# Two more first products inside retention, own banks for the first k, and raw weights touched three steps behind their load

## The chip, the cores and the metric

The kernel runs on one core of one Trainium2 chip. The metric is the device time of one execution in microseconds (us); the kernel before takes 892.86 us, the median of three runs. PE is TensorE, DVE VectorE, ACT ScalarE, POOL GpSimd, SP the engine that issues most of the DMAs.

## The reference

Retention (attention with a decay in place of the softmax) over 4 batches, 8 heads, 576 positions, head size 64, followed by two feed-forward layers on the 2304 tokens it leaves:

```python
scores = scale * np.matmul(q, k.transpose(0, 1, 3, 2))
ret = scores * Dmat                      # Dmat: gamma ** (i - j) at and below the diagonal, else 0
x = np.matmul(ret, v)                    # -> 2304 tokens x 512
h = x @ w_in                             # moe: 512 -> 2048
x = (h * np.tanh(softplus(h))) @ w_out   # mish, 2048 -> 512
g = x @ w_gate; val = x @ w_val          # moe2: 512 -> 1536
out = (g * sigmoid(g) * val) @ w_out2    # 1536 -> 512
```

q, k and v are 32-bit floats; the weights come as 64-bit floats.

## The kernel before, in words

Every product of the feed-forward layers is made in three passes: a matrix is split into a rounded upper part and the lower part that is left, and upper x upper, upper x lower and lower x upper are added up in PSUM.

**Retention** (`retention`) runs over 20 steps t: in each of 4 batches five chunks of 128, 128, 128, 128 and 64 positions. A step t makes scores (`scores`, L505), masks them on DVE into p (L515), transposes k of step t + 1 and q of a later chunk through the PSUM tile `tt` (`turn`, L436), adds the state's part and the own part to the output o (L575, L585), updates the state (L549), and lets DVE scale o into x (L598). POOL scales v for the next step (L493). The first 384 tokens of x are split into `xs` (L365 on ACT, L370 on POOL).

**Weights.** w_in and w_out come in 32 blocks of 512 KB (16 each), in the order of the list `todo`; block j lands in one of `RAW = 4` raw tiles (`fetch`, L102). A block becomes a unit by these operations: `rebias` (ACT L114, DVE L115: a shift), `sign` (DVE L119), `join` (DVE L123), and `part` (ACT L133 casts the upper part, then L134 subtracts for the lower part; POOL does it in retention, DVE in the slots). A raw tile is free for block j + 4 when the part of block j is made. In retention a step does at most one such row of operations, in a step of `REST` none, for at most `NA = 18` units; `rebias` there is done for a block that was loaded two converting steps earlier (`seen`).

**First products.** `g1(s)` multiplies tokens by block i of w_in (12 matmuls, L682), `mish` and `g_hi` (ACT L733, L740) and `g_lo` (DVE L744) make g from it, `g2(s)` multiplies g by block i of w_out and adds into four accumulators (12 matmuls, L716). In retention `g1` runs at the steps of `EARLY`, its mish, `g_hi` and `g_lo` one step later. After retention `slot(s)` does, for s from len(EARLY) to 31, one `g1(s)` and one `g2(s - 4)`, then mish and g, and behind them in the queues the conversions: as many as are needed to have 2s units, and then 1 or 2 more (`weights`). Slots 0 to 15 are the first 384 tokens and slot 16 begins the next; unit 28 is the block of w_out that `g2(12)` reads, which stands first in slot 16. In `todo` the blocks are ordered so that slot s needs units 2s - 4 and 2s - 3.

**Behind them** come the remaining products, with sums of weight blocks made on DVE and written to DRAM (`plain1`, `third`, `second`) while the slots run. All queues run in the order in which the program is written.

Of the kernel before, what the change touches and what calls it, by code (L numbers as in the profile page):

```python
# [7 lines left out]
F32 = mybir.dt.float32  # L8
# [9 lines left out]
def retention_mish_swiglu(  # L18
# [33 lines left out]
    RATES, AHEAD = (2.9, 3.3, 0.4, 1.28, 0.9, 1.0), 45  # L52
    EARLY = (9, 11, 14, 17)
    REST = (9, 14, 18, 19)

# [327 lines left out]
    def retention(g1, mish, g_hi, g_lo):  # L383
        with ExitStack() as c0:
# [40 lines left out]


            def turn(name, *items):
                items = [x for x in items if x]
                if not items:
                    return  # L430
                p = ps1.tile([128, 2, 2, NP, 64], F32, tag="tt", name=f"t{name}")
                for z, (n, src, _) in enumerate(items):
                    for pr in range(NP):
                        for r in range(-(-n // 64)):
                            own = slice(64 * r, min(64 * r + 64, n))
                            nc.tensor.transpose(p[:, r, z, pr, :own.stop - own.start], src(pr)[own], ident[own, own])  # L436
                for z, (_, _, empty) in enumerate(items):
                    empty(p[:, :, z])

            def q_item(b, g, e, eng=nc.scalar.copy):  # L440
# [42 lines left out]
            def q_next(t):  # L483
                b, sc, n = steps[t]
                due = (b, 1, sc) if sc < 2 else (b, 2, 0) if sc == 2 else (b + 1, 0, sc - 3)
                return q_item(*due) if b or sc > 1 else None

# [80 lines left out]
            def output(t):  # L568
                b, sc, n = steps[t]
                o = ps1.tile([128, NP, 128], F32, tag="o", name=f"o{t}")  # L570
                if sc:
                    for pr in range(NP):
                        for e in range(2):
                            own = slice(64 * e, 64 * e + 64)
                            nc.tensor.matmul(  # L575
                                o[own, pr, :n], lhsT=sbd[:, pr, own], rhs=q_cols(t)[:, pr],
                                start=(pr == 0), stop=False, skip_group_check=True,
                            )
                state(t)
                if t == 1:  # L580
                    turn("q0_1", q_item(0, 1, 0), q_item(0, 1, 1))
                state_out(t)
# [51 lines left out]
            warm(W[1])  # L634
            turn("k0", k_item(0))
            scale_v(0)
            warm(W[2])
            for t in range(len(steps)):
                scores(t)
# [12 lines left out]
                if on:  # L652
                    join(stage[2])
                    stage[2] += 1
                if conv:
                    if stage[1] < seen[0]:
                        rebias()
                    seen[:] = seen[1], stage[0]
                if x:
# [10 lines left out]
                if conv:  # L670
                    load_next(NA)
            while stage[3] < stage[2]:
                part(NA)

    with tc.manual_schedule():
# [70 lines left out]
        def slot(s):  # L746
# [20 lines left out]
            if s < F1 + OFF and not parts:  # L767
                for _ in range(1 + s % 2):
                    run(weights(n1, True))
            if s == len(EARLY):  # L770
                plain1(0)
            if s % 2 and s > len(EARLY) and s // 2 - 1 < F1 // 2:
                plain1(s // 2 - 1)
            if stage[3] >= n1:
# [297 lines left out]

        FIN1 = (6, 8, 8, 8, 6, 6, 6)
        for s in range(len(EARLY), NS):
            slot(s)
            if s == NS - F1 + 2:
                ya, yb = ysteps("e0", xt[NC], xt[NC + 1])
                ahead += ya + yb[0] + yb[1]
            if s > NS - F1 + 2:
                pop(ahead, 1 + s % 2)  # L1080
            if s >= NS - F1 + 10:
                stream1(s - (NS - F1 + 10))
# [329 lines left out]
```

## Time and profile before

| | |
|---|---|
| median of 3 runs | 892.86 us (890.14 to 893.03) |
| the profiled execution | 894.11 us, its span 892.3 us |
| PE busy | 871.9 us, 98% of the span |
| DVE, ACT, POOL busy | 652.9, 426.6, 53.1 us |
| granted clock of TensorE, mean | 0.998 |

The span runs from the first to the last instruction; the time of the execution is 1.8 us longer. Busy times are sums over stages with different limits, so where a change falls matters: retention lasts to about 106 us, the slots in which weights are still converted to about 161 us.

### The profile page before, as it was taken

The numbers are of one execution on the slowest core, as the hardware profiler recorded it, in microseconds if no ns is written. First come the engines' busy times: TensorE is split into PE (matmuls) and PEld (weight loads), VectorE is DVE, ScalarE is ACT, GpSimd is POOL, SyncE is SP. The second block draws the span as 40 slices with busy tenths as digits, with TensorE's granted clock in tenths as the row PEclk, the third lists the DMA queues.
The fourth block names the chain that finished last, engine by engine and source line by source line (L and its number), as shares of the span: only waits on it lengthen the run. The fifth ranks groups of instructions, "written<-read, shape, count | busy, mean of one in ns | idle before, by whom it ended". The sixth has DMA issues, their size and how long they took to land.

```text
span 892.3 us, 16688 instructions
## 1 busy us (share of the span) xinstructions
PE 871.9 (98%) x6330; PEld 842.0 (94%) x6330; DVE 652.9 (73%) x1271; ACT 426.6 (48%) x835; POOL 53.1 (6%) x47
## 2 busy tenths in 40 slices
PE   7888999999999999999999999999999999999998
PEld 7777899999999999999999999999999999999998
DVE  3886788998777786777786878876676776575772
ACT  3776566645656556565664424263212263222260
POOL 3654300000000000000000000000000000000000
PEclk9999999999999999999999999999999999999999
DMA  9999578577899985799978698978877878877773
GB/s 210 253 231 250 155 209 263 177 236 252 303 325 315 338 285 165 235 335 342 320 269 280 214 335 310 306 245 274 295 251 244 250 252 270 291 256 252 251 246 119
DMA packets 161600, 232.21 MB, mean 260 GB/s; under 512 B 48240, under 2 KB 124272, under 8 KB 161520
## 3 DMA queue, kind: packets, MB, share of 16 engines
q1 hardware_dynamic: 159984, 229.94, 81.4%
q10 hardware_dynamic: 1536, 1.21, 0.5%
q8 instruction: 50, 0.82, 0.4%
q14 instruction: 30, 0.25, 0.1%
HBM read 178.68 MB, written 52.43 MB: 259 GB/s over the span
## 4 chain that ended last, share of the span: by engine, by line
PE 85%; DVE 5%; DMA 5%; ACT 3%; issue 1%; POOL 1%; SPq 0%; ACTq 0%; POOLq 0%; DVEq 0%
PE t L904 29%; PE T L1298 15%; PE te L904 12%; PE e0a L975 7%; PE e1a L975 6%; PE h L682 5%; PE acc L716 4%; DMA raw<-in_moe_w_out_dram 3%; PE s L505 1%; DMA raw<-in_moe_w_in_dram 1%; PE o L585 1%; PE acc L950 1%; DMA v<-in_v_dram 1%; PE idle L630 1%; PE o L575 1%
## 5 line engine op out<-in xcount | busy, mean ns | idle before, releaser
L904 PE MATMUL t<-y,su 128*128 128x384 f32 x1512 | 267.6, 337 | 0.7 <-DVE u L911 0.4
L904 PEld LDWEIGHTS t<-y,su 128*128 128x128 f32 x1512 | 263.8, 188 | 2.9 <-DVE u L911 0.7
L904 PE MATMUL te<-ye,eu 128*128 128x384 f32 x672 | 136.1, 337 | 0.5 <-DVE scratch L911 0.5
L1298 PE MATMUL T<-su,g 128*128 128x256 f32 x1134 | 135.7, 282 | 0.0
L1298 PEld LDWEIGHTS T<-su,g 128*128 128x128 f32 x1134 | 135.6, 190 | 0.0
L904 PEld LDWEIGHTS te<-ye,eu 128*128 128x128 f32 x672 | 113.5, 188 | 5.0 <-DVE scratch L911 0.7
L975 PE MATMUL e1a<-ge,u 128*128 128x512 f32 (+1 forms) x384 | 76.2, 337 | 0.0
L975 PE MATMUL e0a<-ge,u 128*128 128x512 f32 (+1 forms) x384 | 76.1, 337 | 0.0
L682 PE MATMUL h<-xs,u 128*128 128x384 f32 x384 | 72.2, 337 | 0.0
L975 PEld LDWEIGHTS e1a<-ge,u 128*128 128x128 f32 x384 | 61.9, 188 | 6.0
L975 PEld LDWEIGHTS e0a<-ge,u 128*128 128x128 f32 x384 | 62.0, 188 | 5.8
L682 PEld LDWEIGHTS h<-xs,u 128*128 128x128 f32 x384 | 66.8, 188 | 0.3
L716 PE MATMUL acc<-g,u 128*128 128x384 f32 x336 | 63.4, 337 | 1.5 <-DVE u L134 0.9
L716 PEld LDWEIGHTS acc<-g,u 128*128 128x128 f32 x336 | 58.6, 188 | 2.4 <-DVE u L134 1.5
L1167 ACT ACTIVATE sg<-sg 128x384 f32<-128x384 f32 x54 | 28.4, 525 | 58.5 <-DVE sg L911 58.5
L1196 ACT COPY p<-t 128x384 f32<-128x384 f32 x35 | 16.5, 473 | 80.7 <-PE t L904 80.7
L1130 ACT CAST g<-ga 128x384 fp32r<-128x384 f32 x72 | 32.5, 514 | 43.2 <-DVE ga L1175 32.4
L911 DVE TENSOR_TENSOR u<-t,p 128x384 f32<-128x384 f32 x36 | 20.1, 557 | 40.3 <-PE t L904 40.2
L914 DVE TENSOR_TENSOR g<-ga,g 128x384 fp32r<-128x384 f32 x72 | 36.2, 553 | 6.4 <-ACT g L1130 6.2
L911 DVE TENSOR_TENSOR scratch<-te,scratch 128x384 f32<-128x384 f32 x48 | 26.7, 555 | 13.0 <-PE te L904 10.3
L911 DVE TENSOR_TENSOR v<-t,p 128x384 f32<-128x384 f32 x36 | 20.1, 557 | 17.0 <-PE t L904 16.9
L114 ACT ACTIVATE raw<-raw 128x512 f32<-128x512 f32 x32 | 22.1, 692 | 17.7 <-DMA raw<-in_moe_w_out_dram 12.5
(169 smaller groups left out, 1199.5 us busy)
## 6 DMA issues: line engine op xcount, KB each, us to landing
su<-comb SPq DMA_DIRECT2D x126, 512.0 KB, 4.3
su<-fcomb SPq DMA_DIRECT2D x63, 512.0 KB, 4.2
eu<-ecomb SPq DMA_DIRECT2D x56, 512.0 KB, 5.5
comb<-c SPq DMA_DIRECT2D x48, 256.0 KB, 4.8
raw<-in_moe_w_in_dram SPq DMA_DIRECT2D x16, 512.0 KB, 5.8
raw<-in_moe_w_out_dram SPq DMA_DIRECT2D x16, 512.0 KB, 5.4
ecomb<-e SPq DMA_DIRECT2D x32, 256.0 KB, 2.8
ecomb<-u SPq DMA_DIRECT2D x24, 256.0 KB, 4.6
```

The costliest lines, as they stand in the source:

```text
L114: nc.scalar.activation(hi.bitcast(F32), hi.bitcast(F32), AF.Copy, scale=2.0 ** -112)
L505: nc.tensor.matmul(s[:n, e, pr, :n], lhsT=kT[t][64 * e:64 * e + 64, pr, :n], rhs=q_cols(t)[64 * e:64 * e + 64, pr], start=True, stop=True,)
L682: nc.tensor.matmul(ps, lhsT=u[:, a, kk * 128:(kk + 1) * 128], rhs=s[:, e, :], start=(c == 0), stop=(c == n - 1),)
L716: nc.tensor.matmul(accs[b][d][:, :T], lhsT=u[:, a, d * 128:(d + 1) * 128], rhs=g[:, e, :], start=(i == 0 and c == 0), stop=(i == F1 - 1 an ...
L904: nc.tensor.matmul(p, lhsT=w[:, (high, 1 - high)[a], kk * 128:(kk + 1) * 128], rhs=y[kk][:, x, :], start=begin and kk == 0 and (a, x) == ( ...
L911: nc.vector.tensor_tensor(out=out_, in0=a, in1=b_, op=ALU.add)
L914: nc.vector.tensor_tensor(out=out_, in0=a, in1=b_, op=ALU.subtract)
L975: nc.tensor.matmul(o, lhsT=u[:, a, d * 128:(d + 1) * 128], rhs=y[:, :512] if r == 0 else y[:, 512:], start=f == 0 and (a, x) == (0, 0) and ...
L1130: nc.scalar.copy(out=gt[n, c, i][:, 0], in_=x)
L1167: nc.scalar.activation(x, bank_ if part_ is None else x, AF.Silu)
L1196: (nc.scalar.copy if n or i or z else nc.vector.tensor_copy)(out=r["p1"], in_=p)
L1298: nc.tensor.matmul(p[m], lhsT=g[:, x, m * 128:(m + 1) * 128], rhs=w[:, 1 - a, :], start=begin and i == 0 and (a, x) == (0, 0) and not (sha ...
```

## The change

1. The first k is transposed into two PSUM tiles of its own (`first_k`, tags o and st) and copied out by ACT and DVE, half each; before it went through `tt` behind the first q.
2. The second q chunk of batch 0 is turned in two pieces, one with k of step 2 and one ahead of the state update of step 1, instead of both behind it.
3. `EARLY` has six steps, 8, 10, 12, 14, 16, 18, instead of four; `REST` has five. The slots begin at s = 6, and `g2(0)` and `g2(1)` stand in front of them. Slots up to 8 run two conversions behind their g instead of one or two by turns, and plain weights are sent one odd slot later.
4. In retention a block is rebiased when it was loaded three or more steps earlier (`asked`), from step 3 on.

```diff
-    EARLY = (9, 11, 14, 17)
-    REST = (9, 14, 18, 19)
+    EARLY = (8, 10, 12, 14, 16, 18)
+    REST = (9, 13, 17, 18, 19)
...
+            def halves(n, src, to):
+                for pr in range(NP):
+                    for r in range(-(-n // 64)):
+                        own = slice(64 * r, min(64 * r + 64, n))
+                        nc.tensor.transpose(to(r, pr)[:, :own.stop - own.start], src(pr)[own], ident[own, own])
...
+            def first_k():
+                n, src, _ = k_item(0)
+                p = [ps1.tile([128, NP, 64], F32, tag=tag, name=f"tk0_{tag}") for tag in ("o", "st")]
+                halves(n, src, lambda r, pr: p[r][:, pr])
+                kT[0] = at.tile([128, NP, 128], F32, tag="kT", name="kT0")
+                for r, copy in enumerate((nc.scalar.copy, nc.vector.tensor_copy)):
+                    copy(out=kT[0][:, :, 64 * r:64 * r + 64], in_=p[r])
...
-                due = (b, 1, sc) if sc < 2 else (b, 2, 0) if sc == 2 else (b + 1, 0, sc - 3)
-                return q_item(*due) if b or sc > 1 else None
+                due = (b, 1, sc if b else 0) if sc < 2 else (b, 2, 0) if sc == 2 else (b + 1, 0, sc - 3)
+                return q_item(*due) if b or sc else None
...
+                if t == 1:
+                    turn("q0_1", q_item(0, 1, 1))
                 state(t)
-                if t == 1:
-                    turn("q0_1", q_item(0, 1, 0), q_item(0, 1, 1))
...
-            turn("k0", k_item(0))
+            first_k()
...
-                if conv:
-                    if stage[1] < seen[0]:
-                        rebias()
-                    seen[:] = seen[1], stage[0]
+                if conv and t > 2 and stage[1] < asked[t - 3]:
+                    rebias()
...
+                asked.append(stage[0])
+            seen[0] = asked[-2]
...
-                for _ in range(1 + s % 2):
+                for _ in range(2 if s < len(EARLY) + 3 else 1 + s % 2):
                     run(weights(n1, True))
...
-            if s % 2 and s > len(EARLY) and s // 2 - 1 < F1 // 2:
-                plain1(s // 2 - 1)
+            if s % 2 and s > len(EARLY) and s // 2 - 2 < F1 // 2:
+                plain1(s // 2 - 2)
...
+        for s in range(len(EARLY) - LAG):
+            g2(s)
         for s in range(len(EARLY), NS):
             slot(s)
```

What this does to the order on the engines is shown at three places. In names, the digits up to the underscore say which step, block or product it is, the rest is a running number; lines of the changed kernel lie 12 or 13 further down from retention on.

First DVE in retention, steps 2 to 5, before: x is the scaled output of a step, p the masked scores, raw0 and raw1 the first raw blocks.

```order
L598 TENSOR_TENSOR x0_314<-o2_440,gout_186 128x4x128
L115 TENSOR_SCALAR raw0_324<-raw0_324 128x512
L515 TENSOR_TENSOR p3_487<-s3_478,mask_184 128x2x256 x2
L119 SCALAR_TENSOR_TENSOR raw0_324<-raw0_324 128x512
L598 TENSOR_TENSOR x1_539<-o3_512,gout_186 128x4x128
L123 SCALAR_TENSOR_TENSOR raw0_324<-raw0_324 128x512
L115 TENSOR_SCALAR raw1_406<-raw1_406 128x512
L515 TENSOR_TENSOR p4_562<-s4_553,mask_184 64x2x2x64 x2
```

The same place now:

```order
L610 TENSOR_TENSOR x0_316<-o2_442,gout_186 128x4x128
L527 TENSOR_TENSOR p3_487<-s3_478,mask_184 128x2x256 x2
L610 TENSOR_TENSOR x1_538<-o3_511,gout_186 128x4x128
L115 TENSOR_SCALAR raw0_326<-raw0_326 128x512
L527 TENSOR_TENSOR p4_560<-s4_551,mask_184 64x2x2x64 x2
L119 SCALAR_TENSOR_TENSOR raw0_326<-raw0_326 128x512
L610 TENSOR_TENSOR x1_538<-o4_587,gout_186 128x4x64
L123 SCALAR_TENSOR_TENSOR raw0_326<-raw0_326 128x512
L115 TENSOR_SCALAR raw1_408<-raw1_408 128x512
```

The shift of raw0 (L115) stood behind the x of step 2 and now stands behind that of step 3, and each later block moves a step with it.

Second SP's queue from the load of k for step 8 on, before (q, k, v are loads for retention, raw a weight block):

```order
L418 DMA k8_620<-in_k_dram 128x8x64
L102 DMA raw4_622<-in_moe_w_in_dram 128x4x256
L418 DMA v8_691<-in_v_dram 128x8x64
L405 DMA q10_693<-in_q_dram 128x8x128
L418 DMA k9_695<-in_k_dram 64x8x64
L102 DMA raw5_697<-in_moe_w_out_dram 128x1024
L418 DMA v9_774<-in_v_dram 64x8x64
L418 DMA k10_776<-in_k_dram 128x8x64
```

The same place now:

```order
L418 DMA k8_615<-in_k_dram 128x8x64
L418 DMA v8_684<-in_v_dram 128x8x64
L405 DMA q10_686<-in_q_dram 128x8x128
L418 DMA k9_688<-in_k_dram 64x8x64
L102 DMA raw4_690<-in_moe_w_in_dram 128x4x256
L418 DMA v9_767<-in_v_dram 64x8x64
L418 DMA k10_769<-in_k_dram 128x8x64
L102 DMA raw5_771<-in_moe_w_out_dram 128x1024
```

Block 4 has moved behind v8, q10 and k9, and every later block is behind loads that it stood ahead of; in front of v19 stand blocks 0 to 11 now, 0 to 13 before.

Third DVE where retention ends, before: x5 is the last output, g4 the lower part of the products 4 and 5, u the lower part of a unit.

```order
L598 TENSOR_TENSOR x5_1538<-o19_1696,gout_186 128x4x64
L744 TENSOR_TENSOR g4_1762<-m4_1760,g4_1762 128x384
L119 SCALAR_TENSOR_TENSOR raw13_1469<-raw13_1469 128x512
L115 TENSOR_SCALAR raw14_1545<-raw14_1545 128x512
L123 SCALAR_TENSOR_TENSOR raw13_1469<-raw13_1469 128x512
L744 TENSOR_TENSOR g4_1762<-m5_1799,g4_1762 128x384
L119 SCALAR_TENSOR_TENSOR raw14_1545<-raw14_1545 128x512
L134 TENSOR_TENSOR u13_1804<-raw13_1469,u13_1804 128x512
L115 TENSOR_SCALAR raw15_1626<-raw15_1626 128x512
L123 SCALAR_TENSOR_TENSOR raw14_1545<-raw14_1545 128x512
L119 SCALAR_TENSOR_TENSOR raw15_1626<-raw15_1626 128x512
```

The same place now:

```order
L610 TENSOR_TENSOR x5_1552<-o19_1700,gout_186 128x4x64
L757 TENSOR_TENSOR g4_1623<-m5_1718,g4_1623 128x384
L757 TENSOR_TENSOR g6_1794<-m6_1792,g6_1794 128x384
L115 TENSOR_SCALAR raw10_1396<-raw10_1396 128x512
L119 SCALAR_TENSOR_TENSOR raw10_1396<-raw10_1396 128x512
L115 TENSOR_SCALAR raw11_1470<-raw11_1470 128x512
L123 SCALAR_TENSOR_TENSOR raw10_1396<-raw10_1396 128x512
L134 TENSOR_TENSOR u10_1805<-raw10_1396,u10_1805 128x512
L119 SCALAR_TENSOR_TENSOR raw11_1470<-raw11_1470 128x512
L115 TENSOR_SCALAR raw12_1557<-raw12_1557 128x512
L123 SCALAR_TENSOR_TENSOR raw11_1470<-raw11_1470 128x512
L134 TENSOR_TENSOR u11_1814<-raw11_1470,u11_1814 128x512
```

Before, retention left 13 units (0 to 12) with their parts, and blocks 13 to 15 go on here, one sign and one shift further; now it leaves 10, and blocks 10 to 12 have everything still to be done here, behind the g of product 6.

## Rows read from the trace of the kernel before

**Rows 1.** busy by stage: us, engines' busy (instructions), clock, DMA share, GB/s
```profile
0.00:11.76 11.76, 8.06 (x61) 7.48 (x61) 1.87 (x3) 3.09 (x4) 1.38 (x6) 1.00 1.00 195
11.76:54.60 42.84, 37.03 (x688) 32.44 (x688) 32.06 (x48) 27.44 (x55) 27.35 (x23) 1.00 1.10 245
54.60:106.43 51.83, 47.48 (x781) 42.43 (x777) 38.54 (x60) 35.08 (x68) 24.39 (x20) 0.97 0.87 209
106.43:160.81 54.38, 52.88 (x300) 51.99 (x301) 44.13 (x82) 33.83 (x61) 0.00 (x0) 1.00 0.75 233
160.81:230.00 69.19, 69.19 (x400) 69.19 (x400) 61.74 (x125) 39.10 (x76) 0.00 (x0) 1.00 0.71 231
```

**Rows 2.** waits of PE up to 160 us: us in total, times, longest
```profile
PE o L585 <- DVE p L515: 8.1, 9, 2.2
...
PE s L505 <- DVE qT L456: 1.3, 2, 0.9
```

**Rows 3.** timeline of the start: start, us, engine, line [idle before <-releaser]
```profile
8.62 1.40 DVE L456 COPY qT<-tq 64x512 f32<-64x512 f32 x2 [7.23 <-ACT qT L456]
...
10.28 0.47 PE L436 MATMUL tk<-ident,k 64*128 64x64 f32 x8 [2.10 <-DVE qT L456]
...
11.76 1.16 PE L505 MATMUL s<-qT,kT 64*128 64x128 f32 x16
```

**Rows 4.** chain that ended last, up to 165 us: start us, us, what
```profile
43.20 7.41 DMA raw<-in_moe_w_out_dram
...
144.02 5.61 DMA raw<-in_moe_w_out_dram
```

**Rows 5.** timeline of all engines in retention, 50 to 56 us
```profile
51.11 0.43 DVE L115 TENSOR_SCALAR raw<-raw 128x512 uint32<-128x512 uint32 x1 [1.57 <-DMA raw<-in_moe_w_out_dram]
...
54.10 2.02 DVE L123 SCALAR_TENSOR_TENSOR raw<-raw 128x512 uint32<-128x512 uint32 x1
...
54.25 1.31 POOL L134 TENSOR_TENSOR u<-raw,u 128x512 fp32r<-128x512 f32 x1
```

**Rows 6.** timeline of PE at the end of retention and in the slots
```profile
106.36 2.35 PE L682 MATMUL h<-xs,u 128*128 128x384 f32 x12
108.54 2.24 PE L716 MATMUL acc<-g,u 128*128 128x384 f32 x12
110.62 2.24 PE L682 MATMUL h<-xs,u 128*128 128x384 f32 x12
...
158.79 2.19 PE L716 MATMUL acc<-g,u 128*128 128x384 f32 x11 [0.61 <-DVE u L134]
```

**Rows 7.** timeline of DVE in the slots
```profile
109.81 0.56 DVE L744 TENSOR_TENSOR g<-m,g 128x384 fp32r<-128x384 f32 x1 [2.91 <-ACT g L740]
110.29 0.69 DVE L119 SCALAR_TENSOR_TENSOR raw<-raw 128x512 uint32<-128x512 uint32 x1
...
114.45 0.69 DVE L119 SCALAR_TENSOR_TENSOR raw<-raw 128x512 uint32<-128x512 uint32 x1
115.05 0.69 DVE L134 TENSOR_TENSOR u<-raw,u 128x512 fp32r<-128x512 f32 x1
115.65 0.42 DVE L115 TENSOR_SCALAR raw<-raw 128x512 uint32<-128x512 uint32 x1
115.99 0.69 DVE L123 SCALAR_TENSOR_TENSOR raw<-raw 128x512 uint32<-128x512 uint32 x1
...
117.42 0.69 DVE L134 TENSOR_TENSOR u<-raw,u 128x512 fp32r<-128x512 f32 x1
...
127.96 0.56 DVE L744 TENSOR_TENSOR g<-m,g 128x384 fp32r<-128x384 f32 x1 [0.59 <-ACT g L740]
...
158.05 0.69 DVE L134 TENSOR_TENSOR u<-raw,u 128x512 fp32r<-128x512 f32 x1
```

**Rows 8.** timeline of the DMA queue of SP in retention
```profile
87.72 1.21 SPq L418 DMA_DIRECT2D k<-in_k_dram  x1
```

**Rows 9.** DMA issues up to 110 us: count, KB each, median us to landing
```profile
k<-in_k_dram SPq DMA_DIRECT2D x16, 256.0 KB, 6.2
```

More of the change, by code (lines that the diff above doesn't have):

```diff
@@ L432, in turn @@
                 for z, (n, src, _) in enumerate(items):
[L433 to L436, printed above, removed]
+                    halves(n, src, lambda r, pr: p[:, r, z, pr])
                 for z, (_, _, empty) in enumerate(items):
                     empty(p[:, :, z])
+            def first_k():
[5 more added lines that the diff above has]
+                    copy(out=kT[0][:, :, 64 * r:64 * r + 64], in_=p[r])
             def q_item(b, g, e, eng=nc.scalar.copy):
@@ L634, in retention @@
             warm(W[1])
-            turn("k0", k_item(0))
+            first_k()
             scale_v(0)
             warm(W[2])
+            asked = []
             for t in range(len(steps)):
```

## The prediction

> **What bounds the kernel now.** I read the busy time by stage first [rows 1]. From 160.81 us on TensorE (PE) is busy for the whole stretch to 230 us, so anything that delays PE before that point is paid one for one at the end. The idle time lies ahead of it. Up to 106.43 us (retention) PE is busy 8.06 + 37.03 + 47.48 = 92.6 us and idle 13.9; in the slots up to 160.81 us it is idle 1.5. The share of the whole span (98%) hides this.
>
> Then the waits of PE [rows 2]: 8.1 us in nine waits of the output matmuls for the masked scores p, which VectorE (DVE) writes, and 1.3 us for the q copies. Next the start [rows 3]: the first k transposes wait 2.10 us until the q copies have emptied their bank, and scores begin at 11.76 us.
>
> Why p is late shows in one example [rows 4, 5]: a raw block issued at 43.20 us lands 7.41 us later; DVE gets to it at 51.11 us after a wait of 1.57 us, and p stands behind it in the same queue. A touch one step later would fall at about 54.10 us, when the block is there.
>
> Retention's loads are a second limit: 245 GB/s at a DMA share of 1.10 from 11.76 to 54.60 us [rows 1].
>
> In the slots [rows 6] PE alternates products of 2.08 us (108.54 to 110.62). The last wait that ends there is at 158.79 us, for a lower part written on DVE at 158.05 us [rows 6, 7]. That is unit 28, read by the first second product of slot 16. So the time of the kernel is set by when DVE has converted unit 28, and the whole change comes down to this: when is that unit ready afterwards?
>
> **The change, part by part.** R is the end of retention on PE, 106.36 us before [rows 6]; R' is the same point after.
>
> *First k in own banks.* The 2.10 us wait goes. The first half of k is copied on ScalarE (ACT) while DVE still copies q to 10.02 us (8.62 + 1.40) [rows 3]; the other half takes some 0.4 us behind it (an estimate: half the columns of one q copy, 0.70). Scores can start at about 10.45 instead of 11.76: 1.3 us.
>
> *Two more first products.* Each is 2.28 us of PE (the 2.35 of its row less what overlaps its neighbours) [rows 6]: +4.6 us in retention, and 4.2 us less in the slots. By itself that is no gain; it only pays where PE would have been idle.
>
> *Touch three steps behind.* PE's busy time in retention becomes 92.6 + 4.6, less about 1.5 because the stretch to 106.43 us ran at a granted clock of 0.97 [rows 1]: 95.7. The start's idle time, 11.76 - 8.06 = 3.7, becomes 2.4, and so R' cannot be under 98.1. Of the other 10.2 us of idle I keep 3 (copies, the mish chain, early loads): **R' = 101**. If every wait stayed, R' would be 106.4 + 4.6 - 1.3 = 109.7. Are the loads in the way? SP's order shows that fewer raw blocks now stand ahead of the same q, k, v loads: 12 instead of 14 ahead of the last v. The last k, issued at 87.72 us, moves some 2 x 0.52 MB / 245 GB/s = 4.3 us forward and lands about 6.2 us after issue [rows 1, 8, 9], near 90 us, before its step. So the loads do not hold the end of retention.
>
> *What the later touch costs.* A raw tile is now held one step longer, there are still four of them, and five steps instead of four convert nothing. GpSimd (POOL) therefore makes the lower part of 10 units in retention instead of 13. Units 10, 11 and 12 are still to be touched at all. These three conversions have no cover: they go to the slots, where DVE was the engine waited for.
>
> *The first slot.* DVE stands still longer. Before, its first conversion step came at 110.29 us, 3.93 us after the first product began at 106.36 [rows 6, 7]. Now two second products (4.16 us) come ahead of that product, and the conversions still stand behind its mish in DVE's queue: R' + 8.1. From there I add up DVE's new order with the distances of its old rows: 0.60 us each for sign, join and part, 0.34 for the shift (115.65 to 115.99), 0.48 for g (109.81 to 110.29), and 0.83 between the end of a join and the part of the same unit (115.99 + 0.60 to 117.42, while ACT casts) [rows 7].
> Unit 10: 0.34 + 0.60 + 0.34 + 0.60 + 0.83 + 0.60 = 3.3, done at R' + 11.4. Unit 11 and unit 12: 3.0 each, R' + 17.4. Unit 13: shift, join, g, sign, shift, join, part and 0.3 for its cast: 3.9, R' + 21.3. Before, unit 13 was done at 115.05 + 0.60 = R + 9.3. The chain starts 12 us later relative to the end of retention.
>
> *From unit 13 to unit 28.* Before: 115.05 to 158.05, 43.0 us for 15 units. It holds six waits of 0.6 us for g of a product that PE had not finished (the one at 127.96 us is a sample) [rows 7]; these end when PE is the late one, which gives 39.4. Loads into the four tiles hold it too: one stood in the chain for 5.61 us [rows 4], and this does not get better. I take the middle, 41.2. Bounds: DVE's own work alone, 15 units x (3 x 0.60 + 0.34) + 10 g x 0.48 = 36.9, and 43.0.
>
> *Also changed at no cost:* the sends of plain weights one slot later (SP is not waited for), the split turn for the second q block (saves part of the 1.3 us of [rows 2], counted above).
>
> **Sum.** Unit 28 is done at R' + 21.3 + 41.2 = 101 + 62.5 = 163.5, before at 158.05 + 0.60 = 158.65: 4.8 us later, and everything behind it is unchanged. The profiled execution took 894.1 us, which is 1.2 above the median 892.9; on the median: **897.5 us**. Ends: 98.1 + 21.3 + 36.9 = 156.3, 2.4 us sooner (890.5); with R' at 106.4 and 43.0, 170.7, 12 us later (905).
>
> One price more can be read in two ways. The join at 54.10 us takes 2.02 us while POOL works on a part from 54.25 [rows 5]; in the slots, without POOL, the same operation takes 0.69 [rows 7]. Three POOL parts fewer could so free DVE in retention by up to 3 x 1.31 us. I take nothing for it: PE's long waits there end with a load. The Trainium skill, page "SBUF — State Buffer", section "Who interferes with whom", says that a DVE instruction with two SBUF inputs and a GpSimd instruction that reads SBUF block each other for a whole instruction. By that rule the gain is real, R' falls to its floor, 98.1, and the time is 894.6. The trace agrees that the join is stretched, 2.02 against 0.69 us.
>
> **The rivals.**
> (1) *Not slower: DVE at its own pace in the slots.* If loads never hold it and waits for g vanish, units 13 to 28 take 36.9 us: 101 + 58.2 = 159.2, 0.5 us later: 893.4; with R' at its floor 890.5. For it: four tiles were kept filled at 233 GB/s in that stretch, under the 245 of retention [rows 1]. Against: a load's 5.61 us in the chain [rows 4]. It decides from about 2.6 us per unit down (forecast 2.75, before 2.87).
> (2) *Retention is not shortened.* PE waits as before, now for k and v or for ACT, which has two more mish and casts to do: R' near 106. 106 + 62.5 = 168.5: 902.7. For it: DMA is full to 54.60 us. Against: the raw blocks that are no longer loaded, and the example of [rows 4, 5].
> (3) *DVE in retention is freed* by the missing POOL parts: R' = 98.1, 160.6, 2 us later: 894.6, no change that can be told.
>
> **How the numbers follow.** Forecast 0.5, its own range 894.5 to 901; rival 1 0.22; rival 2 0.16; rival 3 0.12. About 0.3% (2.7 us) is what a measurement of this kernel can tell. Faster by more needs rival 1 with an early R': 0.16. Within it: the rest of rival 1, rival 3 and the low edge of the forecast: 0.24. Slower: 0.60. The range leaves out about one in ten on each side: 889.5 to 904.
>
> **What would show it.** Scores begin near 10.5 us. No wait of DVE for a raw load in retention. PE ends retention between 98 and 104 us, with six first products in it. DVE idle some 7 us around that point; its first shift about 8 us after it. PE waits for u in nearly every slot from slot 7 on, some 15 us in all instead of 1.5 (62.5 us less two second products and ten slots of 4.16); the last wait ends near 163 us, and PE is without gaps behind it. I would be wrong if PE's waits in the slots sum to under 11 us with retention ending by 100, or if PE still waits 8 us for p in retention.

## The result, and the profile after

The changed kernel takes 901.22 us (median of four runs, 899.64 to 902.06), the kernel before 892.70 on the same chip (four runs, 890.14 to 893.03): a ratio of 1.0098, 95% interval 1.0080 to 1.0117, so 8.5 us slower. The profiled executions took 901.48 and 894.11 us; the difference between these two, 7.4 us, is the one that the rows can explain. The median of before in these four runs lies 1.4 us under its profiled execution, that of the changed kernel 0.3 under its own; this is the other 1.1.

Stages of the changed kernel (us, then busy us of each engine with its instructions, granted clock, DMA share, GB/s), as in [rows 1]:

```profile
0.00:10.46 10.46, 7.82 (x61) 7.28 (x61) 2.29 (x4) 2.89 (x4) 1.25 (x5) 1.00 0.97 193
10.46:54.00 43.54, 39.72 (x734) 35.22 (x734) 29.81 (x46) 28.27 (x57) 27.73 (x24) 1.00 1.11 245
54.00:103.60 49.60, 47.61 (x755) 43.34 (x755) 34.43 (x53) 31.48 (x63) 18.20 (x16) 0.97 0.81 191
103.60:166.20 62.60, 52.05 (x269) 46.85 (x265) 48.98 (x90) 34.41 (x61) 0.00 (x0) 0.97 0.65 202
```

The reader sees retention end on PE at 103.60 us instead of 106.36 with two first products more in it, and the slots stretch to 62.6 us with PE idle for 10.5 of them, where it was idle 1.5 before.

Waits of PE up to 103.6 us in the changed kernel (us in total, times, longest), to be held against [rows 2]:

```profile
PE t L431 <- DMA k<-in_k_dram: 3.3, 4, 1.0
...
PE o L597 <- DVE p L527: 0.5, 1, 0.5
```

The waits for p, 8.1 us before, are down to 0.5. Waits for loads of k, of which there were none, stand in their place, 3.3 us.

PE's timeline in the changed kernel: the start, the last late k and the first product behind it, the end of retention, the first unit that came late, and the last:

```profile
10.46 1.16 PE L517 MATMUL s<-qT,kT 64*128 64x128 f32 x16 [1.19 <-DVE kT L450]
...
56.35 0.46 PE L431 MATMUL t<-ident,k 64*128 64x64 f32 x8 [0.95 <-DMA k<-in_k_dram]
...
56.99 3.92 PE L695 MATMUL h<-xs,u 128*128 128x384 f32 x12
...
103.60 4.43 PE L729 MATMUL acc<-g,u 128*128 128x384 f32 x24
...
114.58 4.20 PE L695 MATMUL h<-xs,u 128*128 128x384 f32 x12 [2.39 <-ACT u L133]
...
166.21 2.19 PE L729 MATMUL acc<-g,u 128*128 128x384 f32 x11 [0.68 <-DVE u L134]
```

The last row answers to that at 158.79 us in [rows 6]: the same product, first of slot 16, waits for the same unit 28, 7.42 us later. Profiled time less this row is 901.48 - 166.21 = 735.27 us here and 894.11 - 158.79 = 735.32 before. So the time behind slot 16 did not change; all of the loss is in front of it.

DVE's timeline behind the end of retention and at unit 28, as in [rows 7] (L757 the lower part of g, L115 the shift, L134 the lower part of a unit):

```profile
111.21 0.56 DVE L757 TENSOR_TENSOR g<-m,g 128x384 fp32r<-128x384 f32 x1 [6.60 <-ACT g L753]
111.69 0.42 DVE L115 TENSOR_SCALAR raw<-raw 128x512 uint32<-128x512 uint32 x1
...
114.56 0.69 DVE L134 TENSOR_TENSOR u<-raw,u 128x512 fp32r<-128x512 f32 x1 [0.71 <-ACT u L133]
...
124.07 1.50 DVE L134 TENSOR_TENSOR u<-raw,u 128x512 fp32r<-128x512 f32 x2
...
165.47 0.69 DVE L134 TENSOR_TENSOR u<-raw,u 128x512 fp32r<-128x512 f32 x1
```

DVE stands still for 6.60 us ahead of the g of product 6 (111.21), touches unit 10 at 111.69 (8.1 us behind the end of retention), begins its part at 114.56, that of unit 13 at 124.07 (the row merges it with that of unit 14), and that of unit 28 at 165.47.

### The profile page after: what moved, and what is told of

Its sections match the earlier page's. It is cut to its first block, busy times and chain, and to the rows that moved or that the text cites. A ratio compares the mean times of both kernels' runs of the same rounds, so it can differ in the third digit from the quotient of the medians.

```text
span 899.7 us, 16678 instructions
## 1 busy us (share of the span) xinstructions
PE 875.6 (97%) x6330; PEld 842.2 (94%) x6330; DVE 653.9 (73%) x1275; ACT 426.3 (47%) x835; POOL 47.2 (5%) x44
## 4 chain that ended last, share of the span: by engine, by line
PE 86%; DVE 6%; DMA 3%; ACT 2%; issue 1%; SPq 1%; DVEq 0%; ACTq 0%
PE t L917 29%; PE T L1313 15%; PE te L917 12%; PE e0a L988 7%; PE e1a L988 6%; PE h L695 6%; PE acc L729 4%; DMA raw<-in_moe_w_out_dram 2%; PE o L597 1%; DMA k<-in_k_dram 1%; PE s L517 1%; PE o L587 1%; PE acc L963 1%; DVE raw L123 1%; PE t L431 1%
## 5 line engine op out<-in xcount | busy, mean ns | idle before, releaser
L695 PE MATMUL h<-xs,u 128*128 128x384 f32 x384 | 77.3, 350 | 4.5 <-ACT u L133 2.7
L695 PEld LDWEIGHTS h<-xs,u 128*128 128x128 f32 x384 | 69.2, 196 | 7.8 <-ACT u L133 3.8
L757 DVE TENSOR_TENSOR g<-m,g 128x384 fp32r<-128x384 f32 x32 | 18.4, 575 | 15.8 <-ACT g L753 15.6
```

What stands on the lines that cost most here:

```text
L695: nc.tensor.matmul(ps, lhsT=u[:, a, kk * 128:(kk + 1) * 128], rhs=s[:, e, :], start=(c == 0), stop=(c == n - 1),)
L757: nc.vector.tensor_tensor(out=g[:, 1, :], in0=ws.pop(s), in1=g[:, 0, :].bitcast(F32), op=ALU.subtract)
```

## The experiments

All times are medians of four to twelve runs, each beside runs of the kernel before on the same chip; the chips differ, so kernels are compared by their ratios; "last wait" is the row of the first second product of slot 16, and R' the end of retention on PE, both of the profiled execution. The theories: **A**, the units that retention leaves undone are the loss, because DVE begins them late and has no room to catch up; **B**, the two added first products are; **C**, the later touch brings nothing in retention; **D**, the pace of DVE or of the loads in the slots, and not the start, sets the end.

| kernel | time, us | ratio to before (95%) | R' | last wait | units from retention |
|---|---|---|---|---|---|
| before | 892.70 | 1 | 106.36 | 158.79 | 13 |
| changed | 901.22 | 1.0098 (1.0080 to 1.0117) | 103.60 | 166.21 | 10 |
| e1: changed, old touch | 897.07 | 1.0062 (1.0049 to 1.0074) | 105.79 | 161.85 | 12 |
| e3: before, new touch | 895.35 | 1.0040 (1.0026 to 1.0053) | 99.89 | 158.74 | 10 |
| e4: changed, conversions first | 895.02 | 1.0035 (1.0023 to 1.0048) | 102.79 | 159.81 | 10 |
| e6: e1, conversions first | 891.17 | 0.9992 (0.9981 to 1.0003) | 104.43 | 154.80 | 12 |
| e2: before, first k and split q | 890.77 | 0.9985 (0.9975 to 0.9995) | 104.32 | 155.78 | 13 |
| e8: e6, late parts on POOL | 894.49 | 1.0025 (1.0014 to 1.0036) | 106.33 | 161.21 | 12 |
| e9: e1, two steps in every slot | 898.13 | 1.0071 (1.0056 to 1.0085) | 104.69 | 153.39 | 12 |
| e10: e9, 13 units from retention | 895.19 | 1.0028 (1.0018 to 1.0039) | 104.06 | none | 13 |
| e11: e10, xs first | 886.48 | 0.9943 (0.9928 to 0.9958) | 106.08 | none | 13 |
| e12: e11, slot 13 empty too | 887.09 | 0.9952 (0.9938 to 0.9966) | 107.00 | none | 13 |
| e13: changed, k ahead of q | 899.83 | 1.0094 (1.0080 to 1.0108) | 102.03 | 164.85 | 10 |
| e14: changed, with all of it | 893.68 | 1.0016 (1.0002 to 1.0030) | 103.55 | 154.80 | 10 |

Before, e3 and e2 have four first products in retention and so 4.2 us more of PE behind R' than the others. R' is that of a single execution: e10, e11 and e12 have the same retention and end it at 104.06, 106.08 and 107.00 us, so a difference of one to three us in R' between two kernels is not shown by it alone. Profiled executions also differ in where they lie: those of e8, e11 and e12 are the slowest of their runs, that of e9 the fastest. In e14 the last wait is for unit 27. In the nine kernels whose last wait is for unit 28 and that have no wait behind it at slot 16, the profiled time less that row is 734.8 to 735.3 us, whatever was changed in front.

**e1, the changed kernel with the old touch.**

```diff
-            asked = []
...
-                if conv and t > 2 and stage[1] < asked[t - 3]:
-                    rebias()
+                if conv:
+                    if stage[1] < seen[0]:
+                        rebias()
+                    seen[:] = seen[1], stage[0]
...
-                asked.append(stage[0])
-            seen[0] = asked[-2]
```

> The changed kernel with the old rule for the touch (two converting steps behind the load); six first products and own banks stay. By its order retention leaves 12 units instead of 10. Theory A (the loss is that DVE converts too late after retention: start behind slot 6, and fewer units done): DVE's waits for raw loads come back in retention, so it ends later than 103.6, near 106.5 us; unit 13 is done about 15.0 us after that instead of 21.1 and unit 28 near 163, against 166.1: 897 us, 894 to 900. Theory B (two more first products in retention are the loss as such, units do not matter): no gain, and the raw waits come on top: 902 to 905.

Measured 897.07 us, as theory A had it; DVE waits for raw blocks in retention again, 4.7 us in all. **e3, the kernel before with the new touch alone** (the same lines the other way round):

> The kernel before with only the touch three steps behind the load; four first products, k through the shared bank. Retention leaves 10 units instead of 13. Theory A: retention ends near 100.3 us (103.6 less two products of 2.28, plus 1.3 for the start), six earlier than before, and the chain of conversions is three units longer behind it, some 8 us: unit 28 near 159.3 against 158.65 before, so the gain is eaten: 893.5 us, 890 to 897. Theory C (the touch brings nothing, loads hold retention): it ends near 106 and the three units cost 8 us in full: 901.

Measured 895.35 us. PE in e3, the end of retention and the last wait:

```profile
99.89 2.37 PE L683 MATMUL h<-xs,u 128*128 128x384 f32 x12
...
158.74 2.19 PE L717 MATMUL acc<-g,u 128*128 128x384 f32 x11 [0.56 <-DVE u L134]
```

C falls: the touch alone ends retention 6.5 us sooner (99.89 against 106.36). But unit 28 comes at the same time, 158.74 against 158.79: the slots give all of it back, since three units more are done there. In the medians e3 is 0.4% slower; its profiled execution, 893.96 us, lies at the low end of its runs (893.92 to 895.84), that of before near the high end of its own. B alone doesn't explain the loss either: going back to the old touch, with the six products kept, takes the ratio from 1.0098 to 1.0062, 3 of the 8.5 us.

**e4 and e6: the units that PE needs next are converted ahead of slot 6**, so DVE need not wait for the mish of product 6. In e4 (on the changed kernel) units 10 and 11, in e6 (on e1, with `2 * len(EARLY) + 2` in the added line) units 12 and 13:

```diff
         for s in range(len(EARLY) - LAG):
             g2(s)
+        while stage[3] < 2 * len(EARLY):
+            run(weights(n1))
```

> The changed kernel with the conversions of units 10 and 11 written ahead of slot 6, so that DVE does them while it stood still for 6.6 us. Theory A: unit 13 is done about 15.3 us after the end of retention instead of 21.1, and the whole kernel gains those 5.8 us: 895.5 us, 893 to 898. Theory D (the pace of the chain through the four raw tiles decides, not its start): unit 28 is ready at the same time and the kernel takes 901.

> Both: the old touch rule (12 units from retention) and units 12 and 13 converted ahead of slot 6. Theory A: unit 13 is done about 7 us after the end of retention, unit 28 about 48 us after it, close to PE's own 45.9 us; with retention ending near 106.5 unit 28 is ready near 154.5 against 158.65 before: 888.6 us, 885 to 893, faster than both. Theory B: two more products in retention cannot pay: 893 or more.

Measured 895.02 and 891.17 us. DVE in e6, the parts of unit 13 and of unit 28, then PE's last wait:

```profile
110.66 0.69 DVE L134 TENSOR_TENSOR u<-raw,u 128x512 fp32r<-128x512 f32 x1 [0.73 <-ACT u L133]
...
154.06 0.69 DVE L134 TENSOR_TENSOR u<-raw,u 128x512 fp32r<-128x512 f32 x1
```
```profile
154.80 2.20 PE L728 MATMUL acc<-g,u 128*128 128x384 f32 x11 [0.56 <-DVE u L134]
```

Unit 13 is done at R' + 6.8 (110.66 + 0.60 - 104.43, with 0.60 us for a part as in the prediction) and not at R' + 21.1 as in the changed kernel, unit 28 at R' + 50.2 and not at R' + 62.5. Moving work that is not less in amount ahead of one wait brings some 6 us in both kernels (897.07 to 891.17; the ratio 1.0098 to 1.0035). D falls: from unit 13 to unit 28 pass 43.4 us in e6 and 41.4 in the changed kernel, so the pace is no better, and the place where the chain starts decides. e6 lies 2.6 us above the time that was named for it and ties with the kernel before.

**e2, the kernel before with the first k in own banks and the split q turn, nothing else.**

> The kernel before with the first k in own banks and the split q turn alone; touch, counts of first products and slots stay as before. Theory A (the start only shifts retention): scores begin near 10.46 us as in the changed kernel, instead of 11.76, the end of retention on PE comes at 105.1 instead of 106.36, the last wait in the slots near 157.5 instead of 158.79, and the time is 1.3 us under that of the kernel before. Rival (the loads, not PE, set the pace of retention, so an earlier start is waited away on the next raw block): scores at 10.46, end of retention within 0.4 us of 106.36, last wait within 0.4 of 158.79, no difference in time. 0.6 us or less separates the two.

Measured 890.77 us, 1.47 less than before beside it, as theory A had it. PE in e2:

```profile
11.12 1.16 PE L517 MATMUL s<-qT,kT 64*128 64x128 f32 x16 [1.21 <-DVE kT L450]
...
104.32 2.35 PE L694 MATMUL h<-xs,u 128*128 128x384 f32 x12
...
155.78 2.18 PE L728 MATMUL acc<-g,u 128*128 128x384 f32 x11 [0.44 <-DVE u L134]
```

In this execution scores begin later than expected (11.12, not 10.46), retention ends 2.0 us sooner and the last wait 3.0; with the spread of R' that is no finer answer than the medians give. By the ratio this part of the change brings some 1.3 us (0.4 to 2.2 by its interval), near the 1.3 of theory A.

**e8, e6 with the lower parts of the slots on POOL instead of DVE.**

```diff
         if late:
-            part(lim, nc.vector)
+            part(lim)
```

> The kernel that keeps the first k, the six first products and the old touch and converts all twelve touched units ahead of slot 6 (891.17 us, last wait 154.80), with one edit: in the slots the lower part of a unit is written by POOL instead of by VectorE. Theory P (POOL only takes 0.60 us of each of some 14 units off VectorE, which is busy 43.7 of 50.4 us there): VectorE's chain runs ahead of PE, the last wait ends near 150.5 to 152, the time is 886.5 to 888.5. Rival L (VectorE's sign and join, which read SBUF, are held while POOL reads, as the join of 2.02 instead of 0.69 us in retention suggests, and the part itself takes longer on POOL): the join in the slots rises from 0.69 toward 1.3 to 2 us, the last wait ends at 156 to 164, the time is 892.5 to 900.

Measured 894.49 us: a ratio of 1.0025 where e6 has 0.9992, 2.9 us. DVE's groups from 104 to 161 us in e8 (count, busy us, mean ns of one, idle before), then the same groups in e6:

```profile
L119 DVE SCALAR_TENSOR_TENSOR raw<-raw 128x512 uint32<-128x512 uint32 x18 | 14.6, 809 | 0.0
L115 DVE TENSOR_SCALAR raw<-raw 128x512 uint32<-128x512 uint32 x18 | 13.5, 749 | 4.9 <-DMA raw<-in_moe_w_out_dram 4.2 <-DMA raw<-in_moe_w_in_dram 0.6
L123 DVE SCALAR_TENSOR_TENSOR raw<-raw 128x512 uint32<-128x512 uint32 x17 | 12.8, 751 | 0.0
```
```profile
L119 DVE SCALAR_TENSOR_TENSOR raw<-raw 128x512 uint32<-128x512 uint32 x20 | 13.7, 686 | 0.0
...
L123 DVE SCALAR_TENSOR_TENSOR raw<-raw 128x512 uint32<-128x512 uint32 x19 | 13.0, 686 | 0.0
L115 DVE TENSOR_SCALAR raw<-raw 128x512 uint32<-128x512 uint32 x19 | 8.1, 424 | 1.5 <-DMA raw<-in_moe_w_out_dram 1.5
```

Beside POOL's parts the shift takes 749 ns in the mean instead of 424 (single ones 1.53 us), the sign 809 instead of 686 (single ones 1.80). DVE lost 5.9 + 2.2 + 1.1 = 9.2 us so, about as much as the parts that it no longer made (15 of 0.60 us, 9.0). In addition a part takes 1.3 to 1.9 us on POOL and units come later; DVE's waits for raw rose from 1.5 to 4.9 us, which fits tiles that come free later. The join, which rival L had named, went up least, from 686 to 751 ns in the mean. The profiled execution of e8, 896.55 us, is the slowest of its twelve, so these sums may lie at the high end. The Trainium skill, page "SBUF — State Buffer", section "Who interferes with whom", names both kinds, a DVE instruction with two SBUF inputs and a `tensor_scalar` in a two-port mode, as ones that contend with GpSimd; this run agrees, 0.69 to 1.80 us for the sign and 0.42 to 1.53 for the shift, though that the shift runs in such a mode is not shown.

**e9 and e10: two conversion steps in every slot, and three ahead of slot 6 in the form in which the part of a unit is made one step later** (so DVE waits for no cast); e10 leaves 13 units from retention (`REST` without step 17).

```diff
+        for _ in range(3):
+            run(weights(n1, True))
...
-                for _ in range(2 if s < len(EARLY) + 3 else 1 + s % 2):
+                for _ in range(2):
```

> The changed kernel with the old touch (897.07 us, last wait 161.85, end of retention 105.79), with two edits: three conversion steps run ahead of slot 6 in their late form, and every slot runs two conversion steps instead of two and one by turns from slot 9 on. Theory A (the start of VectorE's chain is the loss): units are finished early enough that PE hardly waits, the last wait lies 46 to 48 us behind the end of retention, near 152, and the time is 886 to 888.5. Rival (VectorE's or the loads' own pace from unit 13 on is the limit whenever it starts): the last wait stays at 154.5 to 157 us and the time at 890 to 892.5.

> As the run before with one unit more converted in retention (13 lower parts from there, as in the kernel before, instead of 12). If VectorE in the slots is the limit, one unit less there brings 2.1 to 3.0 us of it, less what retention gives for it (0.5 to 1.3): last wait 1 to 2 us sooner than in the run before. If PE is the limit by then, the end of retention is 0.5 to 1.3 us later and so is the time: the same to 1.3 us slower than the run before.

Measured 898.13 and 895.19 us: both miss. The units came in time (in e10 PE waits for none after retention, in e9 for 1.2 us in all), and PE then stood at a place that nobody had looked at. PE in e10 at slots 16 and 17, then ACT ahead of it, then DVE, then windows (start:end, us, busy us of PE, PEld, DVE, ACT and POOL with their instructions, granted clock, DMA share, GB/s):

```profile
152.51 1.21 PE L694 MATMUL h<-xs,u 128*128 128x384 f32 x6
156.71 0.69 PE L694 MATMUL h<-xs,u 128*128 128x384 f32 x1 [2.99 <-ACT xs L365]
159.91 5.81 PE L694 MATMUL h<-xs,u 128*128 128x384 f32 x17 [2.52 <-DVE xs L370]
165.52 2.51 PE L728 MATMUL acc<-g,u 128*128 128x384 f32 x12
```
```profile
155.21 0.65 ACT L133 CAST u<-raw 128x512 fp32r<-128x512 f32 x1 [0.42 <-DVE raw L123]
155.77 0.48 ACT L745 ACTIVATE m<-h 128x384 f32<-128x384 f32 x1
156.15 0.91 ACT L365 CAST xs<-x 128x384 fp32r<-128x384 f32 x2
```
```profile
156.50 1.29 DVE L306 TENSOR_TENSOR e<-u 128x512 f32<-128x512 f32 x2
...
159.31 1.02 DVE L370 TENSOR_TENSOR xs<-x,xs 128x384 fp32r<-128x384 f32 x2
```
```profile
148.40:152.50 4.10, 4.10 (x25) 4.10 (x24) 3.57 (x8) 2.42 (x5) 0.00 (x0) 1.00 1.05 388
152.50:159.90 7.40, 1.90 (x8) 1.19 (x7) 6.97 (x15) 4.16 (x9) 0.00 (x0) 0.73 0.37 131
159.90:163.00 3.10, 3.09 (x10) 3.09 (x11) 0.78 (x3) 1.05 (x3) 0.00 (x0) 0.50 0.00 0
```

The first product of slot 16 takes new tokens. Their split `xs` stands in ACT's queue behind casts of units 30 and 31, which PE needs only in slots 18 and 19. In DVE's queue it stands behind the parts of these units and behind 2.3 us of sums of weight blocks (156.50 to 158.84), which the program begins once all units are converted. In e9 the same two waits are 4.58 and 2.52 us. In e10 they are 5.5 us; after them the 17 matmuls that were left run at a granted clock of 0.50, the lower of its two levels, and take 5.81 us where 24 take 4.33 without the wait. From 152.51 to 165.52 us pass 13.0 us instead of 4.2: the wait costs 8.8, not 5.5.

**e11 and e12: xs ahead of mish and g in slot 15, fewer steps in slots 13 and 14** (e11 one and none, e12 none and none).

```diff
+            for kk in parts:
+                split_hi(d, nm, j, kk)
             mish(s)
-            for kk in parts:
-                split_hi(d, nm, j, kk)
             g_hi(s)
-            g_lo(s)
             for kk in parts:
                 split_lo(d, nm, j, kk, nc.vector)
+            g_lo(s)
...
-                for _ in range(2):
+                for _ in range({F1 - 3: 1, F1 - 2: 0}.get(s, 2)):
```

> The run with 13 units from retention and two late conversion steps in every slot (895.19 us) never waited for a unit in the slots, and lost its gain at the first product of the second block, which waited 2.99 us for the high and 2.52 us for the low halves of xs and then ran at a lower clock. Edits: in slot 15 the two xs casts stand ahead of the mish and their low halves ahead of that of g; slot 13 runs one conversion step and slot 14 none. Theory X (the xs wait comes from conversion steps that stand ahead of the xs in ACT's and DVE's queues): the xs waits go or fall under 1.5 us together, the 24 first products of slots 16 and 17, which took from 152.51 to 165.52 us, take 4.2 to 6 us, and the time is 886 to 889 us. Rival Y (the later units are then late for slots 17 to 19, or the xs wait is set by PE's release of its buffers): waits for u or xs of 3 us or more remain and the time is 891 to 895.

> As the run before, but slot 13 runs no conversion step either, so that three units are left for slots 15 and 16. Theory X: the same 886 to 889 us, within 1.5 us of the run before, the xs waits at most as long. Rival Y: unit 29 comes late for the second product of slot 17, a wait of 0.6 to 3 us, and the time is 1 to 3 us above the run before.

Measured 886.48 and 887.09 us, with theory X. PE in e11, and then in e12:

```profile
154.06 1.21 PE L694 MATMUL h<-xs,u 128*128 128x384 f32 x6
156.02 0.44 PE L694 MATMUL h<-xs,u 128*128 128x384 f32 x1 [0.76 <-ACT xs L365]
156.67 3.26 PE L694 MATMUL h<-xs,u 128*128 128x384 f32 x17 [0.21 <-DVE xs L370]
```
```profile
154.97 4.33 PE L694 MATMUL h<-xs,u 128*128 128x384 f32 x24
```

The waits fall to 1.0 us in e11 and to none in e12, where PE has no gap from the end of retention through slot 17. The order in slot 15 and the fewer steps were not tried apart. e11 is the fastest kernel of the study: 0.57% under the kernel before and, by the ratios, 1.5% under the changed one. It holds the first k in own banks and the six first products, but the old touch. No run has these orders with four first products, so what the two added products bring by themselves is not shown.

**e13, the changed kernel with k loaded ahead of q in each step** tests the term that the prediction left out.

```diff
+                load(t + 4, "k", k)
                 if t == 0:
                     load_q(4)
                 load_q(t + 5)
-                load(t + 4, "k", k)
```

> The changed kernel with k loaded ahead of q in each step. It had waited for k loads four times in retention, 3.3 us, and its end of retention was 103.60 us. Theory K (these waits are the part of retention that the prediction left out): the k waits fall under 1.2 us, the end of retention comes at 101 to 102.2, the last wait 62.5 us behind it, and the time is 1.4 to 2.6 us under that of the changed kernel, 898.5 to 900. Rival (the queue waits for the k buffer's release, or q is late in its place): retention ends at 103.1 or later and the time is within 0.6 us of the changed kernel's 901.2.

In the profiled execution the waits for k are gone (one for q, 0.6 us, is there), R' is 102.03, and the last wait comes 62.8 us behind it, as theory K has it. In time it is 899.83 us; its ratio, 1.0094, cannot be told from the 1.0098 of the changed kernel. And e14, with the same order of loads, waits for k again, 2.3 us. So that late k held PE is shown by the trace of the changed kernel; that this order removes the waits, or that their removal shortens the whole, is not shown.

**e14, the changed kernel with its touch and 10 units, and all that was found above** (e13 with four late steps ahead of slot 6 and the edits of e11).

> The changed kernel with its three-step touch and 10 units from retention, and with all that the runs before found: k loaded ahead of q, four late conversion steps ahead of slot 6, two in every slot but one in slot 13 and none in slot 14, xs ahead of mish and g in slot 15. Beside the run at 886.48 us it differs in the touch, the order of k, and 10 units instead of 13 from retention. Theory A (VectorE is full from the end of retention on, so a unit fewer from retention costs some 2.6 us there): retention ends near 102, four us sooner than there, unit 28 is done some 51 to 53 us behind it, PE waits 4 to 6 us for units in the slots, and the four us are given back: 886 to 889 us. Rival T (the shorter retention is kept, since PE is the limit in the slots): waits for units under 1.5 us together and 882 to 884.5 us. Rival S (raw blocks are late when they are all touched in the slots): 890 us or more.

Measured 893.68 us (twelve runs from 890.43 to 895.78), a miss by 5 us for theory A, whose mechanism is seen nevertheless. DVE in e14 at the parts of units 27 and 28, and PE:

```profile
154.06 1.50 DVE L134 TENSOR_TENSOR u<-raw,u 128x512 fp32r<-128x512 f32 x2
```
```profile
103.55 4.50 PE L729 MATMUL acc<-g,u 128*128 128x384 f32 x24
...
131.94 2.20 PE L729 MATMUL acc<-g,u 128*128 128x384 f32 x11 [0.19 <-DVE u L134]
133.98 2.60 PE L695 MATMUL h<-xs,u 128*128 128x384 f32 x12
...
154.80 4.26 PE L729 MATMUL acc<-g,u 128*128 128x384 f32 x23 [1.04 <-DVE u L134]
158.90 1.38 PE L695 MATMUL h<-xs,u 128*128 128x384 f32 x7
```

Unit 27 is done 51.2 us behind R' and unit 28, the second of the two, 52.0 (51 to 53 expected), and from R' to the first product of slot 16 pass 158.90 - 103.55 = 55.3 us, against 154.06 - 106.08 = 48.0 in e11: the slots take 7.4 us more than where PE has no gap, of which the named waits are only 2.8. Some 0.5 of it is not waiting: the first twelve products behind R' take 25.5 us (103.55 to 129.08) and in e11 25.1 (106.08 to 131.15), without a gap and at a granted clock of 1.00 in both; why, no run shows. Retention is 2.5 us shorter than in e11, not 4; PE waited 2.3 us for k in this execution in spite of the order. Rival S has the time but not its mechanism: DVE's waits for raw blocks are 1.9 us in all. How much of the rest is due to slots 13 and 14, which were set for 13 units, stays open; no run separates it. A fifth raw tile, which would let retention keep loading while blocks are held longer, was not tried.

## Why the prediction was right, point by point

- **The start: right.** 10.45 predicted, 10.46 measured.
- **The end of retention, R' = 101: too low by 2.6 us; this is the term that was mis-sized.** PE's busy time came out (95.7 predicted; 7.82 + 39.72 + 47.61 = 95.2 measured), but not by its reason: the prediction took 1.5 us off for a granted clock of 0.97 that it expected to rise, and the stretch from 54.00 us ran at 0.97 again. What made up for it is not shown, so this term is right in part by luck. Wrong was "Of the other 10.2 us of idle I keep 3": 3.8 + 2.0 = 5.8 us stayed idle behind the start, 3.3 of it for k. "So the loads do not hold the end of retention" was argued from the last k alone; the k that were late are early ones, between 32.28 and 56.35 us, while DMA moves 245 GB/s. In the execution of e13, without these waits, R' is 102.03. (The spread of R' over executions is as large as the miss; within the profiled execution the sum closes.) A part of the busy time goes with these waits too: behind the wait for k at 56.35 us the first product took 3.92 us at a clock of 0.56 instead of 2.35 us.
- **Waits for p: right.** 8.1 us before, 0.5 after, and DVE waits for no raw block in retention.
- **10 units instead of 13: right**, and by e1, e3, e4 and e6 it is the cause of the loss together with the next step.
- **The first slot: right.** First shift at R' + 8.1 (predicted 8.1), unit 10 done at R' + 11.6 (11.4), unit 13 at R' + 21.1 (21.3).
- **Unit 13 to unit 28 in 41.2 us: right, in part by luck.** 166.07 - 124.7 = 41.4; the sum R' + 62.5 came out as R' + 62.5 (166.07 - 103.60). But 41.2 was the middle between all waits for g kept and all gone. Four of these waits are still there, 2.7 us; with 1.4 us of waits for raw loads, 0.3 for casts and the 36.9 of own work they make 41.3.
- **"Everything behind it is unchanged": right** to 0.1 us in the profiled executions (735.27 and 735.32).
- **Rival 1** (DVE at its own pace) fell: that pace would have been 36.9 us. **Rival 2** (retention not shortened) fell as a whole, but its condition, PE waiting for k instead, held: R' came at 103.60, halfway between the forecast's 101 and its 106. **Rival 3** (DVE freed in retention by fewer POOL parts) did not show: R' was 103.6, not 98.1, and the joins in retention were no shorter, 1158 ns in the mean of ten against 1091 of 13 before. That DVE is stretched beside POOL, on which it rests, e8 shows.
- **Waits for u, "some 15 us": right in sum, by lengths of stretches.** 62.6 us less two second products and ten slots (45.8) is 16.8; the waits that the view of waits names add up to 10.2. By that view they lie under the 11 us that the prediction gave as a sign of being wrong; the other half of that sign, retention ending by 100, did not come.

So 4.8 + 2.6 = 7.4 us is the whole difference of the two profiled executions. On the median the forecast was 897.5 (its own terms, 892.86 + 4.8, add up to 897.7, and rival 3's to 894.8, not 894.6). The 901.22 measured lies 3.5 us above that sum: 2.6 from R', and 0.9 because the profiled execution of the changed kernel lies 0.3 above its median and not 1.2, as was taken off. So the mechanism was right and the direction followed from it; the number lies just above the forecast's own range, 894.5 to 901, and nearer to rival 2's 902.7.

## What to carry to other kernels

Work taken out of a stage where it was in the way is no gain when it goes to a stage whose critical engine is that same one: count when the last late item is ready, not when the stage ends. What stands behind a long wait in an in-order queue can matter more than how much there is; here some six us lay in the order around one mish. When such a wait is removed, look for the next item with a deadline in the same queues before adding work there: here the split of the next tokens turned a gain of 0.6% into a loss of 0.3%.

## What the runs showed of the hardware

Windows of the changed kernel around the two products that took 3.92 and 4.20 us instead of 2.24 to 2.35 (columns as in the windows of e10):

```profile
54.00:56.90 2.90, 1.71 (x30) 1.55 (x30) 1.62 (x4) 1.19 (x3) 0.21 (x1) 1.00 1.14 277
56.99:60.84 3.85, 3.85 (x16) 3.60 (x13) 0.65 (x2) 1.71 (x3) 1.04 (x1) 0.56 0.86 237
...
114.58:118.70 4.12, 4.01 (x13) 3.69 (x14) 3.38 (x6) 1.80 (x3) 0.00 (x0) 0.59 0.42 127
118.70:121.00 2.30, 2.30 (x15) 2.19 (x13) 2.15 (x5) 1.21 (x3) 0.00 (x0) 1.00 0.70 205
```

PE had been busy 1.71 of 2.90 us ahead of the first, and waited 2.39 us ahead of the second; the granted clock was then 0.56 and 0.59 in the mean, between its two levels of 0.50 and 1.00, while PE was busy nearly throughout, and 1.00 again behind it. There the wait is paid a second time: 1.6 and 2.0 us here, 2.7 in e10. But not behind every wait. Later in the same trace:

```profile
147.00 0.44 PE L729 MATMUL acc<-g,u 128*128 128x384 f32 x1 [2.05 <-ACT u L133]
147.72 2.18 PE L729 MATMUL acc<-g,u 128*128 128x384 f32 x11 [0.29 <-DVE u L134]
```

Behind these 2.05 us the granted clock stays at 1.00 (147.00 to 149.74 us) and the product runs at full pace, and so it does behind a wait of 1.35 us at 159.00. What tells the two cases apart is not shown. And where a unit is late by a little in every slot, the view of waits names little of it: in e14 the starts of two first products lie 4.9 us apart (129.08 and 133.98) and not 4.16, while the wait named between them is 0.19 us. The lengths of stretches are the safer reading, not the sum of the waits.
